# Weight sums used from the tiles they are made in, their raw words loaded on another queue, and their decoding dealt over all bursts

## The chip, the cores and the metric

The kernel runs on one core of a Trainium2 chip. The metric is the device time of the execution in microseconds (us). The engines are named as in the profile: PE (TensorE, with PEld for its weight loads), DVE (VectorE), ACT (ScalarE), POOL (GpSimd) and SP (SyncE, which here only issues DMAs). Each takes its instructions in the order of the program. PE's granted clock has two levels, 2.4 GHz (shown as 1.00) and 1.2 GHz (0.50).

## The reference

```python
# 8 batches, 12 heads, 448 tokens, head size 64
scores = q @ k.T / sqrt(64) - log(448)
attn = sigmoid(scores) @ v              # (8, 12, 448, 64)
x = attn as (3584 tokens, 768)
a = x @ w1;  b = x @ w2                 # each (768, 1024)
h = (a * b) @ w3                        # (1024, 1024)
out = h @ w_out                         # (1024, 768)
```

q, k and v are float32. The four weights come as 64-bit floating point numbers, which the kernel reads as pairs of 32-bit words and turns into float32 itself.

## The kernel before, in words

**Attention** is worked through in 84 bursts of two items each (the loop over `k` at the end of the first half). An item is a tile of scores (line 173, or the short ones of line 183 for the last 64 keys of two pairs of heads), its sigmoid on ACT (line 163), and one burst later its product with v (lines 196 and 204). Score tiles have two PSUM buffers, so the scores of a burst need the sigmoids of the burst before.

**The bilinear stage**, a and b, is computed for groups of two batches (`up(g)`, four groups). The two batches and the two weights form a 2 x 2 block product, which is done with seven products in place of eight. For each of eight blocks of 128 columns (`fc`) `finish_weights` makes seven weight operands from the float32 blocks `b11`, `b21` (w1) and `b12`, `b22` (w2); I call them sums. Each sum is split into a high and a low part: ACT casts (line 66), DVE subtracts (line 67). A product is 9 matmuls on one sum (line 440): three chunks of the inner dimension times three combinations of high and low. PE's results are added up by DVE (line 419) and ACT (lines 448 and 454), and stored to `g_dram`. A group has 56 products, 504 matmuls.

**Group 0** runs beside bursts 25 to 52: every second burst takes a portion of 36 matmuls, four products. Groups 1 and 2 run in one piece after bursts 58 and 70, group 3 at the end. The remaining weights, w3 and w_out, are decoded in `prepare_rest` beside group 1 and later.

**The weights' way.** `prepare_weights` is a generator: each `next` emits one step. Raw words of one block (768 KB, two tiles in turn) are loaded by SP (line 71). ACT takes the magnitude (line 76), DVE runs six steps (lines 83 to 104) per block of w1 and of w2, and after each step some steps of the block before are popped (`pops`): its sums. So each `fc` has 12 decode steps and 11 more. A step stands for one or two DVE operations, and some have one on ACT. In the last decode step (line 104) the raw tile is read for the last time; the load of the next `fc`'s words into it is issued right behind. The magnitude of these words is taken during the following block.

A sum's parts are written to a `wo` tile (four buffers), POOL stores them to `w_dram` (line 339), and `load_weights` loads them back on SP into a ring of six `w` tiles (line 367), five products ahead of their use. If a sum isn't made by then, `load_weights` runs `next(weights)` until it is.

**The order** of all engines is the order in which the code emits. Before burst 25 one or two weight steps follow each burst, and two bursts before 25 five loads are forced. From burst 25 on steps come only beside products: `beside` takes one unit of `change` (the high and low parts of x) or, if none is left, three or four weight steps.

Of the kernel before, what the change touches and what calls it, by code (L numbers as in the profile page):

```python
# [25 lines left out]
def sigmoid_attention_bilinear_ffn(  # L26
# [39 lines left out]
        hi_engine(out=dst_hi, in_=src)  # L66
        lo_engine.tensor_tensor(out=dst_lo, in0=src, in1=dst_hi, op=ALU.subtract)  # L67

    def load_words(src, pool, bufs=2):
        raw = pool.tile([P, *src.shape[1:-1], 2], U32, name="raw", bufs=bufs)  # L70
        nc.sync.dma_start(out=raw, in_=src)
        return raw

    def magnitude(raw, pool, bufs=2):
# [219 lines left out]

    PRODUCTS = ("A11", "S2", "A12", "S3", "S1", "A22", "S4")

    def prepare_weights():

        def load(fc, i):
            return load_words(words((w1, w2)[i], slice(fc * P, (fc + 1) * P)), p1)  # L300

        extras = iter(())
        raw = [load(0, i) for i in range(2)]
        yield
        nxt = magnitude(raw[0], p1, 3)
        for fc in range(NF):
            fs = []
            for i in range(2):
                f = nxt
                pops = ((2, 2, 2, 1, 1, 0), (1, 0, 1, 0, 1, 0))[i]  # L310
                fs.append(f)
                for step, _ in enumerate(decode(raw[i], f)):
                    if step == 4 and (i, fc) != (1, NF - 1):
                        nxt = magnitude(raw[1 - i], p1, 3)
                    if step == 5 and fc + 1 < NF:
                        raw[i] = load(fc + 1, i)
                    yield
                    for _ in range(pops[step]):
                        if next(extras, None):
                            yield  # L320
            take(extras, 100)
            extras = finish_weights(fc, fs)
        while next(extras, None):
            yield

    def finish_weights(fc, fs):

        b11, b21, b12, b22 = (f[:, h * KH:(h + 1) * KH] for f in fs for h in range(2))

        def subtract(name, in0, in1, out=None):  # L330
            if out is None:
                out = p1.tile([P, KH, P], F32, name=name, bufs=1)
            total(out, in0, in1, ALU.subtract)
            return out

        def divide(k, src):
            wo = p1.tile([P, 2, KH, P], F32R, name="wo", bufs=4)
            split(wo[:, 0], wo[:, 1], src, nc.scalar.copy, nc.vector)
            nc.gpsimd.dma_start(out=w_dram[fc * 7 + k], in_=wo.bitcast(F32))  # L339
            stored.add(fc * 7 + k)  # L340

        divide(0, b11)
        yield 1
        t3 = subtract("t3", b22, b12)
        yield 1
        t1 = subtract("t1", b12, b11, b12)
        yield 1
        divide(2, b21)
        yield 1
        t2 = subtract("t2", b22, t1)  # L350
        yield 1
        n4 = subtract("n4", b21, t2, b21)
        yield 1
        for k, src in ((5, n4), (1, t2), (6, b22), (4, t1), (3, t3)):
            divide(k, src)
            yield 1

    RING = 6
    stored = set()
    ring = {}  # L360

    def load_weights(n):
        if n < NG * NF * 7:
            while n % (NF * 7) not in stored:
                next(weights)
            ring[n] = pm.tile([P, 2, KH, P], F32R, name="w", bufs=RING)
            nc.sync.dma_start(out=ring[n].bitcast(F32), in_=w_dram[n % (NF * 7)])

# [8 lines left out]
    def prepare_rest():  # L377

        raw = {}

        def load(i):
            if i < len(jobs):
                raw[i] = load_words(jobs[i][0], p2[0], 4)

        for i in range(3):
            load(i)
        for _ in range(6):
            yield
        f = magnitude(raw[0], p2[0], 3)
        for i, (_, dst) in enumerate(jobs):  # L390
            load(i + 3)
            for step, _ in enumerate(decode(raw.pop(i), f)):
                if step == 4 and i + 1 < len(jobs):
                    following = magnitude(raw[i + 1], p2[0], 3)
                yield
            nc.gpsimd.dma_start(out=dst, in_=f)
            f = following

    def up(g):

        at = {b: slice(b * S, (b + 1) * S) for b in (2 * g, 2 * g + 1)}
        for fc in range(NF):
# [21 lines left out]

            for k, name in enumerate(PRODUCTS):
                n = (g * NF + fc) * 7 + k
                load_weights(n + RING - 1)
                w = ring.pop(n)
                bank, start, stop = ((0, 1, 0), (1, 1, 0), (0, 0, 1), (1, 0, 1),
                                     (2, 1, 0), (3, 1, 1), (2, 0, 1))[k]  # L430
# [6 lines left out]
                for kc in range(KH):  # L437
                    xh, xl = ops[g][name, kc]
                    for m, (i, x) in enumerate(((0, xh), (0, xl), (1, xh))):
                        nc.tensor.matmul(  # L440
                            a, w[:, i, kc], x, start=bool(start) and kc == 0 and m == 0,
                            stop=bool(stop) and kc == KH - 1 and m == 2, skip_group_check=True,
                        )
                        if (kc, m) != (KH - 1, 2):
                            yield
                if k == 0:
                    p = kept("p")
                    nc.scalar.copy(out=p, in_=a)  # L448
                elif k == 1:
                    u2 = kept("u2")  # L450
                    add(u2, a, p)
                elif k == 2:
                    c11 = kept("c11")
                    nc.scalar.copy(out=c11, in_=a)
                elif k == 3:
                    u3 = kept("u3")
                    add(u3, a, p)
                elif k == 4:
                    c22 = kept("c22")
                    add(c22, a, u3)  # L460
                elif k == 5:
                    add(u3, a, u3)
                    leave(2 * g + 1, u3, c22, u3)
                else:
                    add(u2, a, u2)
                    leave(2 * g, u2, c11, kept("c22"))
# [36 lines left out]

    def beside(g, n):

        if not take(change, 1):
            if g == 0:
                take(weights, 3 + n % 5 % 2)
            else:
                take(rest, 2)  # L510

    qks, splits, vvs = {}, {}, {}
    qks[0] = load_pair(0)
# [45 lines left out]

    for k in range(NBURST + 1):  # L560
        if k == CHANGE:
            take(weights, 10 ** 6)
            phase_1.close()
            p2.append(phase_2.enter_context(tc.tile_pool(name="p2", bufs=2, side="right")))
            rest = prepare_rest()
# [19 lines left out]
        for g, (at, end, stride) in enumerate(spans):  # L585
            if k == at:
                filler = up(g)
            if at <= k < end:
                done = k + 1 - at
                if done % stride == 0:  # L590
                    upto, since = (GROUP * i // (end - at) for i in (done, done - stride))
                    take(filler, upto - since + (10 if k == end - 1 else 0))
                if k == end - 1:
                    change = Units(g + 1)
                break
        else:
            if k < spans[0][0]:
                if k > 2:
                    take(change, 2 if k < 10 else 1)
                    take(weights, 1 if 12 <= k < 23 else 2)  # L600
            else:
                take(change, 3 if k < spans[1][0] else 2)
        if k == spans[0][0] - 2:
            for n in range(RING - 1):
                load_weights(n)
        if k == 1:
            idle_products(6)
    take(filler, 7 * KH * 3 - 9)
# [265 lines left out]
```

## Time and profile before

| | us |
|---|---|
| three runs | 1029.62, 1030.95, 1034.69 (median 1030.95) |
| the profiled execution, its time | 1034.27 |
| its span, first to last instruction | 1032.5 |
| PE busy | 986.9 (96%) |
| DVE busy | 654.1 (63%) |
| ACT busy | 405.5 (39%) |
| POOL busy | 84.6 (8%) |
| mean granted clock | 0.975 |

PE is busy for most of the span, but busy includes the time at the lower clock, in which the same matmuls take twice as long. The idle time of PE and the windows at 0.50 are therefore read together, by stage, and the engines' queues tell what stood ahead of the operation that ended an idle time.

### The profile page before, as it was taken

How to read it: one execution, taken by the hardware profiler on the slowest of the kernel's cores; microseconds unless marked ns; L12 is line 12 of the kernel's file. 1: busy time of each engine (PE TensorE's matmuls, PEld its weight loads, DVE VectorE, ACT ScalarE, POOL GpSimd, SP SyncE). 2: the span in 40 equal slices, each digit the busy share in tenths (PEclk: the TensorE clock that was granted, in tenths of full speed). 3: DMA queues.
4: the chain of work that ended last, by engine and by line, in shares of the span. 5: the costliest groups of instructions: out<-in, count | busy, mean ns of one | idle time of the engine just before them, and what ended most of it. 6: DMA issues, size and time to landing. Idle time of an engine off the chain costs nothing.

```text
span 1032.5 us, 14262 instructions
## 1 busy us (share of the span) xinstructions
PE 986.9 (96%) x5246; PEld 763.1 (74%) x5246; DVE 654.1 (63%) x1051; ACT 405.5 (39%) x591; POOL 84.6 (8%) x156
## 2 busy tenths in 40 slices
PE   9999678988889999999999999999999999999998
PEld 4444455655556589994699964789999999999997
DVE  4786766866532878888788845644445566565563
ACT  6876435543534811118511147211223342323230
POOL 0000111211110001110022100000000000000000
PEclk9999888998889999999999999999999999999999
DMA  7748597997875589995599962598833024343412
GB/s 222 227 130 301 203 340 261 301 311 238 292 263 177 181 272 361 379 377 188 178 354 390 333 209 85 169 320 299 284 130 133 1 99 143 107 144 106 143 37 81
DMA packets 111429, 226.40 MB, mean 219 GB/s; under 512 B 10752, under 2 KB 70144, under 8 KB 111360
## 3 DMA queue, kind: packets, MB, share of 16 engines
q1 hardware_dynamic: 100480, 181.44, 52.6%
q0 software_dynamic: 10880, 44.05, 11.0%
q8 instruction: 42, 0.69, 0.3%
q14 instruction: 27, 0.22, 0.1%
HBM read 170.39 MB, written 55.05 MB: 218 GB/s over the span
## 4 chain that ended last, share of the span: by engine, by line
PE 75%; issue 17%; POOL 3%; DMA 2%; DVE 2%; ACT 1%; SPq 0%; POOLq 0%; ACTq 0%
PE up L440 31%; PE up L839 20%; PE av L196 8%; PE sp L173 7%; PE up L714 6%; POOL w_dram L339 2%; PE sp L183 2%; PE av L204 1%; DMA w<-w_dram 1%; POOL g_dram L423 1%; PE up L488 1%; DMA w_dram<-wo 0%; ACT a L163 0%; DVE A L221 0%; DMA qk<-qT 0%
## 5 line engine op out<-in xcount | busy, mean ns | idle before, releaser
L440 PE MATMUL up<-hS,w 128*128 128x448 f32 x768 | 237.5, 370 | 3.4 <-DVE c L419 2.4
L839 PE MATMUL up<-gh,wo 128*128 128x448 f32 x672 | 192.2, 367 | 0.0
L440 PE MATMUL up<-hA,w 128*128 128x448 f32 x576 | 182.0, 370 | 6.3 <-DVE u L419 5.2
L163 ACT ACTIVATE a<-sp,bias 128x896 f32<-128x896 f32 x168 | 161.4, 1007 | 58.7 <-PE sp L173 55.0
L440 PEld LDWEIGHTS up<-hS,w 128*128 128x128 f32 x768 | 145.2, 189 | 25.1 <-issue 5.4
L440 PE MATMUL up<-lS,w 128*128 128x448 f32 x384 | 141.1, 367 | 0.2 <-DVE lS L67 0.2
L196 PE MATMUL av<-a,vv 128*64 128x448 f32 x576 | 135.4, 586 | 0.0
L839 PEld LDWEIGHTS up<-gh,wo 128*128 128x128 f32 x672 | 126.2, 188 | 11.3
L440 PEld LDWEIGHTS up<-hA,w 128*128 128x128 f32 x576 | 109.2, 190 | 25.1 <-issue 8.0
L839 PE MATMUL up<-gl,wo 128*128 128x448 f32 x336 | 123.2, 367 | 0.0
L440 PE MATMUL up<-lA,w 128*128 128x448 f32 x288 | 105.8, 367 | 0.0
L419 DVE TENSOR_TENSOR u<-up,p 128x448 f32<-128x448 f32 x64 | 39.9, 623 | 91.3 <-PE up L440 91.3
L173 PE MATMUL sp<-high 64*128 64x448 f32 x288 | 64.7, 445 | 26.6 <-ACT a L163 26.6
L173 PEld LDWEIGHTS sp<-high 64*128 64x128 f32 x288 | 28.4, 192 | 82.3 <-ACT a L163 61.3
L196 PEld LDWEIGHTS av<-a,vv 128*64 128x64 f32 x576 | 35.4, 142 | 68.1 <-issue 68.1
L448 ACT COPY p<-up 128x448 f32<-128x448 f32 x32 | 17.1, 534 | 171.4 <-PE up L440 158.8
L440 PEld LDWEIGHTS up<-lS,w 128*128 128x128 f32 x384 | 72.9, 190 | 6.2 <-DVE lS L67 0.5
L839 PEld LDWEIGHTS up<-gl,wo 128*128 128x128 f32 x336 | 63.1, 188 | 5.6
L419 DVE TENSOR_TENSOR u<-up,u 128x448 f32<-128x448 f32 x64 | 39.8, 621 | 40.1 <-PE up L440 39.2
L76 ACT ACTIVATE f<-raw 128x768 f32<-128x768 f32 (+2 forms) x48 | 34.3, 716 | 69.0 <-DMA raw<-w 21.3
L67 DVE TENSOR_TENSOR gl<-gf,gh 128x896 fp32r<-128x896 f32 x40 | 41.9, 1086 | 29.5 <-ACT gh L66 29.5
L67 DVE TENSOR_TENSOR low<-qk,high 128x896 fp32r<-128x896 f32 (+1 forms) x49 | 52.5, 1071 | 11.9 <-ACT high L66 10.9
(83 smaller groups left out, 1313.5 us busy)
## 6 DMA issues: line engine op xcount, KB each, us to landing
w<-w_dram SPq DMA_DIRECT2D x224, 384.0 KB, 5.5
w_dram<-wo POOLq DMA_DIRECT2D x56, 384.0 KB, 5.0
gf<-g_dram SPq DMA_DIRECT2D x16, 896.0 KB, 5.4
raw<-w SPq DMA_DIRECT2D x16, 768.0 KB, 6.1
qk<-qT SPq DMA_DIRECT2D x48, 224.0 KB, 4.8
qk<-kT SPq DMA_DIRECT2D x48, 224.0 KB, 5.2
out<-o_sb SPq DMA_DIRECT2D x48, 224.0 KB, 2.0
vv<-vL SPq DMA_DIRECT2D x24, 384.0 KB, 3.7
```

What stands on the lines that cost most here:

```text
L67: lo_engine.tensor_tensor(out=dst_lo, in0=src, in1=dst_hi, op=ALU.subtract)
L76: nc.scalar.activation(f, raw[..., 1].bitcast(F32), AF.Abs, scale=HW_SCALE)
L163: nc.scalar.activation(dst, src, AF.Sigmoid, bias=bias[:n], scale=scale)
L173: nc.tensor.matmul(sp[:, j], k[rows, 1, at:at + P], q[rows, 0], start=m == 0, stop=m == 2)
L183: nc.tensor.matmul(sp[HEADS[u], j], qk[rows, 1, FULL:], qk[rows, 0], start=True, stop=True)
L196: nc.tensor.matmul(acc[cols, :S], vv[:, c, at:at + D], a[:, j], start=u == 0 and c == 0, stop=u == 1 and c == NC - 2,)
L339: nc.gpsimd.dma_start(out=w_dram[fc * 7 + k], in_=wo.bitcast(F32))
L419: nc.vector.tensor_tensor(out=out, in0=a, in1=b, op=ALU.add)
L440: nc.tensor.matmul(a, w[:, i, kc], x, start=bool(start) and kc == 0 and m == 0, stop=bool(stop) and kc == KH - 1 and m == 2, skip_group_ch ...
L448: nc.scalar.copy(out=p, in_=a)
L714: nc.tensor.matmul(acc, a[:, jc], w[:, jc, ms], start=(jc == 0 and m == 0), stop=(jc == NF - 1 and m == 2),)
L839: nc.tensor.matmul(acc, w[:, fc, ms], g[:, fc], start=start and fc == 0 and m == 0, stop=fc == NH - 1 and m == 2, skip_group_check=True,)
```

## The change

Three things change, and they hang together.

- Group 0 takes each sum from the tile in which it is made. There are ten such tiles in one rotation: the six `w` tiles and the four `wo` tiles (`SLOTS`). A sum is emitted only when the product that used its tile ten sums ago has been emitted (`made`, `used`); otherwise the step yields and does nothing. Sums are still stored to `w_dram`, and groups 1 to 3 load them as before. The first five loads of group 1 are issued at the end of burst 52.
- The raw words of w1 and w2 are loaded from POOL's queue. Those of w3 and w_out stay on SP.
- The steps are dealt differently: two after each burst up to 12, one up to 24, then three in each of the bursts 25 to 52, and two beside each product, in addition to a unit of `change`. Among the last five sums those of `t3` and `b22` trade places.

```diff
-    def load_words(src, pool, bufs=2):
+    def load_words(src, pool, queue, bufs=2):
         raw = pool.tile([P, *src.shape[1:-1], 2], U32, name="raw", bufs=bufs)
-        nc.sync.dma_start(out=raw, in_=src)
+        queue.dma_start(out=raw, in_=src)
...
+    POPS = ((2, 2, 2, 1, 1, 1), (1, 0, 1, 0, 0, 0))
...
-            return load_words(words((w1, w2)[i], slice(fc * P, (fc + 1) * P)), p1)
+            return load_words(words((w1, w2)[i], slice(fc * P, (fc + 1) * P)), p1, nc.gpsimd)
...
-                pops = ((2, 2, 2, 1, 1, 0), (1, 0, 1, 0, 1, 0))[i]
+                pops = POPS[i] if fc else (0,) * 6
...
         def divide(k, src):
-            wo = p1.tile([P, 2, KH, P], F32R, name="wo", bufs=4)
-            split(wo[:, 0], wo[:, 1], src, nc.scalar.copy, nc.vector)
-            nc.gpsimd.dma_start(out=w_dram[fc * 7 + k], in_=wo.bitcast(F32))
-            stored.add(fc * 7 + k)
+            m = len(made)
+            while m >= SLOTS and made[m - SLOTS] not in used:
+                yield False
+            n = fc * 7 + k
+            if m % SLOTS < RING:
+                w = pm.tile([P, 2, KH, P], F32R, name="w", bufs=RING)
+            else:
+                w = p1.tile([P, 2, KH, P], F32R, name="wo", bufs=SLOTS - RING)
+            split(w[:, 0], w[:, 1], src, nc.scalar.copy, nc.vector)
+            nc.gpsimd.dma_start(out=w_dram[n], in_=w.bitcast(F32))
+            ring[n] = w
+            made.append(n)
+            yield True
...
-        for k, src in ((5, n4), (1, t2), (6, b22), (4, t1), (3, t3)):
-            divide(k, src)
-            yield 1
+        for k, src in ((5, n4), (1, t2), (3, t3), (4, t1), (6, b22)):
+            yield from divide(k, src)
...
-            while n % (NF * 7) not in stored:
-                next(weights)
...
-                load_weights(n + RING - 1)
+                if g == 0:
+                    while n not in ring:
+                        next(weights)
+                else:
+                    load_weights(n + RING - 1)
...
+                used.add(n)
...
-        if not take(change, 1):
-            if g == 0:
-                take(weights, 3 + n % 5 % 2)
-            else:
-                take(rest, 2)
+        if g == 0:
+            take(change, 1)
+            take(weights, 2)
+        elif not take(change, 1):
+            take(rest, 2)
...
+                if g == 0:
+                    take(weights, 3)
...
+                    if g == 0:
+                        take(weights, 10 ** 6)
+                        for n in range(RING - 1):
+                            load_weights(NF * 7 + n)
...
-                    take(weights, 1 if 12 <= k < 23 else 2)
+                    take(weights, 2 if k < 13 else 1)
...
-        if k == spans[0][0] - 2:
-            for n in range(RING - 1):
-                load_weights(n)
```

Where the instructions stand shows best at three places. In these rows a name is the tile written and, behind the arrow, the tiles read; L is the line, and x2 means two such rows in a stretch.

The first place is ACT beside the third portion, between one pair of sigmoids (`a`) and the next, before:

```order
L163 ACTIVATE a<-sp,bias 128x896 x2
L284 COPY A_1394<-av 128x448
L66 CAST wo<-f 128x384
L76 ACTIVATE f<-raw 128x768
L66 CAST wo<-t_1330 128x384
L454 COPY c_1433<-up 128x448
L66 CAST wo<-f 128x384 x2
L76 ACTIVATE f<-raw 128x768
L66 CAST wo<-t_1307 128x384
L163 ACTIVATE a<-sp,bias 128x896 x2
```

and now, beside the third portion and the burst behind it:

```order
L284 COPY A_1356<-av 128x448
L66 CAST w<-f 128x384
L469 COPY c_1388<-up 128x448
L66 CAST wo<-f 128x384
L76 ACTIVATE f<-raw 128x768
L66 CAST wo<-t_1390 128x384
L163 ACTIVATE a<-sp,bias 128x896 x2
L66 CAST wo<-t_1358 128x384
L66 CAST high<-qk 128x896
L163 ACTIVATE a<-sp,bias 128x896 x2
```

Two magnitudes and five casts stood between two pairs of sigmoids; now there are one magnitude and three casts, and one cast has moved between the next two pairs.

The second place is SP's queue about burst 23 to 26, before (`raw` are the words of w1 and w2, `w` the sums from DRAM, `qk`, `vv` and `vs` attention's inputs):

```order
L367 DMA w<-w_dram 128x768 x5
L71 DMA raw<-w 128x6x256
L139 DMA vv<-vL 128x3x256
L145 DMA vs<-vL 64x128 x2
L367 DMA w<-w_dram 128x768 x4
L131 DMA qk<-qT 128x448
L131 DMA qk<-kT 128x448
L131 DMA qk<-qT 128x448
L131 DMA qk<-kT 128x448
L367 DMA w<-w_dram 128x768
```

and now, at the same place:

```order
L139 DMA vv<-vL 128x3x256
L145 DMA vs<-vL 64x128 x2
L131 DMA qk<-qT 128x448
L131 DMA qk<-kT 128x448
L131 DMA qk<-qT 128x448
L131 DMA qk<-kT 128x448
```

The sums' loads and the raw words are gone from it; attention's inputs stay in their order.

The third place is the start of POOL's queue, before:

```order
L864 MEMSET const-uint8-127 128x1
L870 UNCONDITIONAL_BRANCH
L339 DMA w_dram<-wo 128x768 x14
L423 DMA g_dram<-u_1160 128x448
L339 DMA w_dram<-wo 128x768
```

and now:

```order
L881 MEMSET const-uint8-127 128x1
L887 UNCONDITIONAL_BRANCH
L71 DMA raw<-w 128x6x256 x4
L352 DMA w_dram<-w 128x768 x4
L71 DMA raw<-w 128x6x256
L352 DMA w_dram<-w 128x768 x2
L352 DMA w_dram<-wo 128x768
```

Four raw loads now come first, and the two first of them wait for nothing; on SP they stood behind the first two pairs of `qk` and the first `vv`.

## Rows read from the trace of the kernel before

**Rows 1.** Stages: stretch, length, busy time by engine (instructions), granted clock, DMA share, GB/s

```profile
97.50:357.10 259.60, 227.18 (x1205) 145.47 (x1203) 160.46 (x264) 126.16 (x187) 36.12 (x65) 0.91 0.75 258
357.10:464.50 107.40, 104.93 (x508) 95.45 (x504) 84.56 (x164) 20.79 (x38) 16.05 (x30) 0.98 0.95 340
316.41:330.22 13.81, 13.81 (x82) 9.69 (x80) 2.96 (x4) 6.15 (x8) 0.54 (x1) 1.00 0.70 228
330.22:357.10 26.88, 26.88 (x171) 15.06 (x169) 20.66 (x35) 18.04 (x28) 1.09 (x2) 1.00 0.52 163
```

**Rows 2.** PE in order of time: start, length, operation [idle before, ended by]

```profile
89.19 0.48 PE L173 MATMUL sp<-high 64*128 64x448 f32 x2 [2.10 <-ACT a L163]
...
128.99 0.74 PE L440 MATMUL up<-hA,w 128*128 128x448 f32 x1 [5.24 <-DVE u L419]
...
155.84 0.74 PE L173 MATMUL sp<-high 64*128 64x448 f32 x2 [6.14 <-ACT a L163]
...
242.75 0.74 PE L173 MATMUL sp<-high 64*128 64x448 f32 x2 [4.31 <-ACT a L163]
...
296.45 0.74 PE L173 MATMUL sp<-high 64*128 64x448 f32 x2 [3.64 <-ACT a L163]
```

**Rows 3.** Windows of the lower clock up to 303 us, columns as Rows 1

```profile
90.95:94.37 3.42, 3.42 (x14) 1.01 (x16) 2.54 (x4) 3.42 (x5) 0.00 (x0) 0.50 0.54 166
...
128.50:131.92 3.42, 2.93 (x8) 2.63 (x9) 3.39 (x6) 0.13 (x1) 1.21 (x3) 0.50 0.48 183
152.39:159.23 6.84, 3.39 (x16) 2.18 (x18) 2.52 (x3) 5.57 (x7) 0.54 (x1) 0.50 0.75 258
...
241.14:247.97 6.83, 5.22 (x20) 2.60 (x20) 2.28 (x3) 5.53 (x8) 0.55 (x1) 0.50 0.98 387
...
295.75:302.59 6.84, 6.14 (x25) 2.65 (x26) 1.02 (x2) 4.09 (x5) 0.43 (x1) 0.50 0.66 261
sum 47.87, PE 40.53 PEld 18.42 DVE 21.14 ACT 30.58 POOL 3.27; mean PE 4.50 PEld 2.05 DVE 2.35 ACT 3.40 POOL 0.36
```

**Rows 4.** ACT's waits from 97.5 to 357.1 us: total, times, longest

```profile
ACT f L76 <- DMA raw<-w: 21.3, 3, 8.3
ACT f L76 <- DVE wo L67: 12.1, 8, 3.4
ACT wo L66 <- DVE f L221: 11.7, 4, 4.3
ACT wo L66 <- DMA w_dram<-wo: 7.2, 3, 3.5
```

**Rows 5.** ACT in order of time, one wait on raw words

```profile
153.59 0.89 ACT L76 ACTIVATE f<-raw 128x768 f32<-128x768 f32 x1 [8.31 <-DMA raw<-w]
```

**Rows 6.** DMAs: raw words in the stage; stores by line (size, median to landing)

```profile
DMA to landing us min/median/max: 4.7/6.1/8.0
...
w_dram<-wo POOLq DMA_DIRECT2D x56, 384.0 KB, 5.0
```

**Rows 7.** The start: DVE and SP in order of time, and stretches as Rows 1

```profile
9.21 0.63 DVE L66 CAST high<-qk 128x896 fp32r<-128x896 f32 x1 [3.66 <-DMA qk<-kT]
...
4.46 1.02 SPq L71 DMA_DIRECT2D raw<-w  x2
...
5.00:6.00 1.00, 1.00 (x7) 0.78 (x8) 0.55 (x1) 0.00 (x0) 0.00 (x0) 1.00 1.03 339
8.00:9.00 1.00, 0.97 (x8) 0.19 (x4) 0.00 (x0) 0.94 (x2) 0.00 (x0) 1.00 0.95 276
```

**Rows 8.** POOL and DVE in order of time, about 145 to 147 us

```profile
145.02 0.54 POOL L339 DMA_DIRECT2D w_dram<-wo  x1 [1.43 <-DVE wo L67]
146.83 0.72 POOL L339 DMA_DIRECT2D w_dram<-wo  x1 [1.27 <-DVE wo L67]
...
146.88 0.55 DVE L89 TENSOR_SCALAR f<-f 128x768 f32<-128x768 f32 x1
```

**Rows 9.** DVE by line in the stage: busy, mean ns, idle before

```profile
L93 DVE SCALAR_TENSOR_TENSOR f<-f,raw 128x768 uint32<-128x768 uint32 x12 | 11.4, 954 | 0.2
```

More of the change, by code (lines that the diff above doesn't have):

```diff
@@ L318, in prepare_weights, with one @@
                     for _ in range(pops[step]):
-                        if next(extras, None):
-                            yield
-            take(extras, 100)
+                        yield from one(extras)
             extras = finish_weights(fc, fs)
-        while next(extras, None):
+        for _ in range(sum(sum(pops) for pops in POPS)):
+            yield from one(extras)
+    def one(extras):
+        while not next(extras):
             yield
+        yield
     def finish_weights(fc, fs):
@@ L336, in divide @@
         def divide(k, src):
-            wo = p1.tile([P, 2, KH, P], F32R, name="wo", bufs=4)
-            split(wo[:, 0], wo[:, 1], src, nc.scalar.copy, nc.vector)
-            nc.gpsimd.dma_start(out=w_dram[fc * 7 + k], in_=wo.bitcast(F32))
-            stored.add(fc * 7 + k)
-        divide(0, b11)
-        yield 1
+            m = len(made)
[11 more added lines that the diff above has]
+            yield True
+        yield from divide(0, b11)
         t3 = subtract("t3", b22, b12)
-        yield 1
+        yield True
         t1 = subtract("t1", b12, b11, b12)
-        yield 1
-        divide(2, b21)
-        yield 1
+        yield True
+        yield from divide(2, b21)
         t2 = subtract("t2", b22, t1)
-        yield 1
+        yield True
         n4 = subtract("n4", b21, t2, b21)
-        yield 1
-        for k, src in ((5, n4), (1, t2), (6, b22), (4, t1), (3, t3)):
-            divide(k, src)
-            yield 1
-    RING = 6
-    stored = set()
+        yield True
+        for k, src in ((5, n4), (1, t2), (3, t3), (4, t1), (6, b22)):
+            yield from divide(k, src)
+    RING, SLOTS = 6, 10
+    made, used = [], set()
     ring = {}
@@ L382, in load @@
             if i < len(jobs):
-                raw[i] = load_words(jobs[i][0], p2[0], 4)
+                raw[i] = load_words(jobs[i][0], p2[0], nc.sync, 4)
         for i in range(3):
@@ L561, in sigmoid_attention_bilinear_ffn @@
         if k == CHANGE:
-            take(weights, 10 ** 6)
             phase_1.close()
```

## The prediction, made before the changed kernel was run

> **What bounds the kernel now.** I read the time by stage first [rows 1]. TensorE (PE) is what the end hangs on, so a change can only give back PE's idle time and the time it runs at the lower of its two clock levels. Nearly all of that lies in one stage: 97.5 to 357.1 us, where group 0's matmuls (line 440) are dealt between the attention bursts. PE is idle there for 259.60 - 227.18 = 32.4 us and the mean granted clock is 0.91. In the stage behind it PE waits 107.40 - 104.93 = 2.5 us, although VectorE (DVE) is busy 84.56/107.40 = 79% of it. So DVE's load alone does not stop PE; in the stage in question it is 62%.
>
> The idle time is eleven gaps between 85 and 303 us, ten of them inside the stage; [rows 2] has those that get a term of their own. Behind most gaps the clock then stands at 0.50 for 3.4 or 6.8 us [rows 3]: nine such windows up to 303 us hold 40.53 us of PE work, which at the full level would take half, so they cost 20.3 us, 1.7 of it before the stage. The stage loses 32.4 + 18.6 = 51.0 us. A cross-check: without them it would take 208.6 us. The stage has 14 portions of 36 matmuls, one every second burst; the last two pieces of [rows 1] are free of gaps, from the thirteenth portion to the last one (13.81 us) and from there to the end (26.88 us), and 13 x 13.81 + 26.88 = 206.4.
>
> Who keeps PE waiting? All ten gaps end with a sigmoid (line 163) or with a DVE operation, both in queues that hold weight work too. So I went to ScalarE (ACT) [rows 4]: 21.3 us for raw words of w1 and w2, 23.8 us for DVE's part of the sums, 7.2 us for the store that still reads one of the four buffers. I sort PE's losses by that:
> - raw words late: gaps 5.24, 6.14, 4.31 (ACT's three waits on raw words stand just before them; [rows 5] is the one before 6.14), 15.7 us, and half the busy time in the windows behind them (2.93, 3.39, 5.22), 5.8 us: **21.5 us**.
> - store buffer: gap 3.64 and half of 6.14: **6.7 us**.
> - the rest of the stage, 51.0 - 21.5 - 6.7 = **22.8 us**: ACT and DVE waiting for each other after a clump of weight steps.
> - the gap at 89 us, ahead of the stage, where the first five weight loads force their sums out in one clump: 2.10 + 3.42/2 = **3.8 us**.
>
> **The change part by part.** Raw words. A raw tile is free when the last decode step (line 104) of its chunk is done, and its new words are wanted at the next magnitude (line 76) on that tile. I counted the PE work that the code's order puts between the two (9 matmuls are 1.9 us, a burst 3.2 us). Before, three to four weight steps go into each product and none into bursts, so for four of the eleven loads that fall into the stage only 0 to 3.7 us lie between; a load takes 6.1 us in the median [rows 6], and three of the four are the three waits above. After, the same count gives 8.2 us at the least and 10.6 in the median, because steps come two to a product and three to each burst, and GpSimd's (POOL's) queue holds only stores that wait for DVE, which has passed them by then. What POOL needs to issue such a load isn't in the trace: its stores with one row per partition take 0.54 us [rows 8], a raw load has six. Bounds: 0.54, and 6 x 0.54 = 3.3 us. Landing is then 6.1 to 9.0 us. I take 7, nearest to the store's 5.0 us [rows 6]; even at 9.0 only the loads with 8.2 and twice 8.7 us are late, by under 1 us, which sigmoids have as slack (ACT's wait of 8.31 us cost PE 6.14). So 21.5 us go.
>
> Sums straight from their tiles. 56 loads of 384 KB leave SP; every tile is finished at least 11 us of PE work before its first matmul by the same count, so PE gets no new wait here. The cast into a tile now waits until PE has read that tile ten sums ago. That is enforced in the code order, and ACT, behind PE's sigmoids anyway, finds it done, except inside a portion, where it has time. Ten buffers in place of four: the stores that hold them were issued long before, and the 6.7 us go. Group 1 is loaded from DRAM as before; its first five loads now come at the end of the portion of burst 52, some 19 us ahead of their use: nothing.
>
> Dealing. A portion of 36 matmuls (7.5 us) had about 14 weight steps beside it and now has 8, with 6 in the two bursts. At 0.55 to 0.95 us of DVE work a step [rows 8, 9], with line 419's sums, the code's order put 9 to 14 us of DVE work beside 7.5 us of PE in the dense portions, and now puts 5 to 9. What is then left over at a portion's end falls, by the same count, from 4 to 10 us to 1.5 to 4. It doesn't vanish, so I leave a third of the 22.8 us in place: 15.2 us go; between 8 and 22.8 is possible. The forced clump at 89 us is gone: 3.8 us.
>
> Start. This is what the change costs. The first two raw loads stood on SP behind both pairs of q and k and the first v; now POOL issues them at once. DVE's cast of the second pair starts the moment its k lands, at 9.21 us [rows 7], and PE's short scores wait for the same landing. The DMA engines are full then (shares 1.03 and 0.95). Two loads of 768 KB at 339 GB/s are 4.6 us. If all of that goes ahead, the landing slips by 4.6 us; if POOL's are served last, by 0. I take 3.7: they queue beside each other from the first microsecond, and a part of the raw words still lands after. From there to 97.5 us PE has one gap only, the one counted above, so nothing takes the slip back. A pause this long brings the lower level: the nearest rows, 2.10 and 3.64 us of idle time, go with windows that cost 3.42/2 = 1.7 and 6.14/2 = 3.1 us; I take 2.4. Together **6.1 us lost**, 0 to 8.
>
> The Trainium skill weighs on this at one place: DMA: Bandwidth & Descriptors, section SWDGE vs HWDGE vs iDMA (Issuing engines are not separate DMA queues), says that DMAs from all issuing engines run on the same 16 engines and interleave. By that the slip at the start is there and the sum stays 993; were it otherwise, it would be 987. The trace fits it (the shares of 1.03 and 0.95), but no row has both queues loading in that stretch.
>
> A second rule speaks against the change. A store took 0.72 us in place of 0.54, and beside it ran a DVE operation with one source tile [rows 8]; a raw load with six rows might so lose 6 x 0.18 = 1.1 us, which is inside the bounds above. The Trainium skill, SBUF — State Buffer, section Summary: rules for kernel authors, says that descriptor generation on GpSimd starves while DVE runs in its faster modes, and to issue from another queue. The 0.18 us agrees in kind; by that rule at full weight the slower rival below would hold.
>
> Sum: 21.5 + 6.7 + 15.2 + 3.8 - 6.1 = 41.1 us. The profiled execution took 1034.27 us (span 1032.5), so 993.2; it lies 3.3 us above the median of 1030.95, so I say **990 us** for the median.
>
> **The rivals.**
> - Half of it stays. ACT and DVE still wait for each other at each portion's end, as they did in gaps where no DMA was late, and some raw words come late because the stage is now denser. Raw 13, store 6.7, rest 6, clump 3.8, start 8: 21.5 us gained, 1009. For it: DVE's load rises to 160/213 = 75%. Against: 79% in the stage behind it, with one gap.
> - All of it comes and the start is free: 51.0 + 3.8 = 54.8, 976. For it: PE has filler matmuls at the start. Against: full DMA engines.
> - Slower: POOL's raw loads are the new wait. With landing at 14.5 us all eleven miss their lead by 3.6 us on average, each costing about 2 us of idle time and 2.4 of clock: 48 us, as much as is won. It decides from there on; at 16 us of landing it gives 1047. Against: POOL's stores land in 5.0 us, SP's raw loads in 8.0 at the worst [rows 6].
> - The change does not do what it says: the waits named on ACT were followers, and PE is held by the sigmoid's own turn. Then the gaps stay and only the start is paid, 1030 to 1036. Against: the last two portions before 357 us, which have no weight work beside them, run without a gap.
>
> **How the numbers follow.** Forecast 0.60 (982 to 1002), half 0.18, all and more 0.09, slower by POOL 0.06, no effect 0.07, split between the last two classes. A measurement of this kernel tells about 0.5%, 5 us, from no change. Faster 0.86, same 0.06, slower 0.08. For 8 in 10 the range takes in the lower bound of the start and of the rest at the fast end (978), and half at the slow end: 978 to 1010.
>
> **What would show it.** Right: PE's idle time from the first portion on falls from 32 us to under 8, the clock there is 0.97 or more, no wait of ACT on raw words over 2 us, the landing of the second k near 13 us, one early window at 0.50. Wrong: ACT waits on raw words again (POOL's issue rows over 3 us, landing over 10), casts that wait for PE, or gaps of 2 to 3 us behind every portion.

## The result, and the profile after

The changed kernel takes 989.33 us (median of four runs, 988.64 to 989.85), the kernel before 1032.12 beside it (1029.62 to 1034.69): ratio 0.9585, 95% interval 0.9558 to 0.9612. The forecast was 990 in 978 to 1010. The profiled execution took 988.85 us, its span is 987.1, against 1034.27 and 1032.5: 45.4 us less.

The two stages of [rows 1], from just before the first matmul of group 0 (97.55 us before, 96.99 now) to the start of group 1, and group 1 (columns as there):

```profile
96.95:313.15 216.20, 211.17 (x1205) 139.68 (x1203) 162.06 (x266) 125.46 (x188) 44.60 (x76) 0.99 0.65 217
313.15:418.35 105.20, 102.80 (x508) 94.57 (x504) 84.63 (x164) 20.78 (x38) 16.29 (x30) 1.00 0.96 348
```

The first stage is 259.60 - 216.20 = 43.4 us shorter. PE is idle there for 5.0 us where it was 32.4, and the clock is 0.99 where it was 0.91; the DMA share fell from 0.75 to 0.65 although the stage is shorter. Group 1 is 2.2 us shorter.

PE in order of time, all pauses of over 1 us behind the first matmul (before: [rows 2]):

```profile
11.16 0.97 PE L183 MATMUL sp<-qk 64*64 64x448 f32 x4 [1.94 <-DMA qk<-kT]
...
118.06 0.62 PE L454 MATMUL up<-hS,wo 128*128 128x448 f32 x1 [2.39 <-DVE c L429]
...
204.82 0.47 PE L454 MATMUL up<-hA,wo 128*128 128x448 f32 x1 [1.07 <-ACT p L463]
...
220.28 0.47 PE L454 MATMUL up<-hS,w 128*128 128x448 f32 x1 [1.12 <-DVE c L429]
...
326.96 0.47 PE L454 MATMUL up<-hS,w 128*128 128x448 f32 x1 [2.40 <-DVE c L429]
```

One more, of 1.27 us, waits for a sum from DRAM in group 3. In place of the nine windows at 0.50 up to 303 us [rows 3] there are two:

```profile
12.41:15.82 3.41, 3.41 (x10) 1.26 (x7) 2.09 (x3) 0.77 (x1) 0.00 (x0) 0.50 0.90 314
118.22:121.64 3.42, 3.42 (x10) 3.05 (x11) 2.08 (x4) 0.00 (x0) 0.77 (x2) 0.50 0.40 161
```

The pause at 11 us and the window behind it are new, and are what the change costs at the start. POOL and DVE there, in order of time (before: [rows 7]):

```profile
1.29 0.98 POOL L71 DMA_DIRECT2D raw<-w  x1 [0.85 <-POOLq L881]
9.60 0.85 POOL L71 DMA_DIRECT2D raw<-w  x1 [7.33 <-DMA raw<-w]
...
11.12 0.63 DVE L66 CAST high<-qk 128x896 fp32r<-128x896 f32 x1 [5.64 <-DMA qk<-kT]
```

The second k lands 1.9 us later than before. The second row was in nobody's forecast: nothing in the program makes POOL's second raw load wait, yet it is issued 7.33 us late, 0.3 us after the first has landed (9.29). ACT's waits in the stage (before: [rows 4]) show raw words still late, though half as long:

```profile
ACT f L76 <- DMA raw<-w: 10.3, 4, 4.3
ACT wo L66 <- DVE f L221: 6.0, 3, 3.5
ACT f L76 <- DVE w L67: 4.4, 5, 1.7
```

So two things were to be settled: which of the three parts brings the gain, and what POOL's queue does.

### The profile page after: what moved, and what is told of

The parts are those of the page before. It is cut to its first block, busy times and chain, and to the rows that moved or that the text cites. A ratio compares the mean times of both kernels' runs of the same rounds, so it can differ in the third digit from the quotient of the medians.

```text
span 987.1 us, 14120 instructions
## 1 busy us (share of the span) xinstructions
PE 968.4 (98%) x5246; PEld 757.0 (77%) x5246; DVE 656.1 (66%) x1051; ACT 403.8 (41%) x591; POOL 98.3 (10%) x172
## 4 chain that ended last, share of the span: by engine, by line
PE 84%; issue 5%; DMA 4%; DVE 4%; POOL 1%; ACT 1%; SPq 1%; POOLq 0%; DVEq 0%; ACTq 0%
PE up L454 33%; PE up L856 21%; PE av L196 10%; PE sp L173 9%; PE up L731 7%; DMA w<-w_dram 3%; PE sp L183 2%; PE av L204 2%; POOL w_dram L352 1%; DMA qk<-kT 1%; DMA raw<-w 1%; DVE u L429 0%; DVE A L221 0%; DVE lS L67 0%; ACT a L163 0%
## 5 line engine op out<-in xcount | busy, mean ns | idle before, releaser
L454 PE MATMUL up<-hS,w 128*128 128x448 f32 x702 | 215.9, 368 | 4.8 <-DVE c L429 3.5
L163 ACT ACTIVATE a<-sp,bias 128x896 f32<-128x896 f32 x168 | 160.6, 1006 | 54.3 <-PE sp L173 48.1
L454 PE MATMUL up<-hA,w 128*128 128x448 f32 x522 | 163.5, 367 | 1.4 <-DMA w<-w_dram 1.4
L454 PEld LDWEIGHTS up<-hS,w 128*128 128x128 f32 x702 | 132.0, 188 | 22.2 <-DVE c L429 4.5
L454 PE MATMUL up<-lS,w 128*128 128x448 f32 x351 | 128.5, 366 | 0.2 <-DVE lS L67 0.2
L196 PE MATMUL av<-a,vv 128*64 128x448 f32 x576 | 128.0, 559 | 0.0
L454 PEld LDWEIGHTS up<-hA,w 128*128 128x128 f32 x522 | 98.1, 188 | 14.2 <-issue 3.5
L454 PE MATMUL up<-lA,w 128*128 128x448 f32 x261 | 95.4, 366 | 0.0
L454 PEld LDWEIGHTS up<-lS,w 128*128 128x128 f32 x351 | 66.0, 188 | 5.5 <-DVE lS L67 0.5
L173 PE MATMUL sp<-high 64*128 64x448 f32 x288 | 62.0, 427 | 0.9 <-ACT a L163 0.9
L66 ACT CAST gh<-gf 128x896 fp32r<-128x896 f32 x40 | 35.8, 943 | 60.2 <-PE up L856 50.0
```

What stands on the lines that cost most here:

```text
L163: nc.scalar.activation(dst, src, AF.Sigmoid, bias=bias[:n], scale=scale)
L173: nc.tensor.matmul(sp[:, j], k[rows, 1, at:at + P], q[rows, 0], start=m == 0, stop=m == 2)
L196: nc.tensor.matmul(acc[cols, :S], vv[:, c, at:at + D], a[:, j], start=u == 0 and c == 0, stop=u == 1 and c == NC - 2,)
L454: nc.tensor.matmul(a, w[:, i, kc], x, start=bool(start) and kc == 0 and m == 0, stop=bool(stop) and kc == KH - 1 and m == 2, skip_group_ch ...
```

## The experiments

Ratios are to the kernel before on the same chip, whose median was 1028.9 to 1034.3 us from one set of runs to the next; 0.001 is 1 us.

### Which part does what

The change has three parts, and each was run without the others, or the others without it.

| dealing | tiles | POOL's queue | run | median, us | ratio and 95% interval |
|---|---|---|---|---|---|
| new | yes | yes | the changed kernel | 989.33 | 0.9585 (0.9558 to 0.9612) |
| new | yes | no | e1_raw_sp | 984.55 | 0.9562 (0.9525 to 0.9600) |
| new | yes | no | e12_raw_sp_again | 984.81 | 0.9527 (0.9496 to 0.9557) |
| new | no | no | e4_new_deal | 1002.64 | 0.9739 (0.9684 to 0.9794) |
| old | yes | no | e6_tiles_only | 1015.58 | 0.9836 (0.9792 to 0.9880) |
| old | yes | yes | e3_old_deal | 1016.66 | 0.9876 (0.9837 to 0.9914) |
| old | no | yes | e5_pool_only | 1046.92 | 1.0142 (1.0099 to 1.0186) |

**e1_raw_sp**, POOL's part undone:

```diff
-            return load_words(words(...), p1, nc.gpsimd)
+            return load_words(words(...), p1, nc.sync)
```

> The changed kernel (989.3 us) with the raw words of w1 and w2 issued by SP again; sums from their tiles and the new dealing stay. Theory A, POOL's queue only costs: the second k lands at about 9.1 us again in place of 11.03, the pause of 1.94 us and the window at 0.50 behind it go (3.5 us), and the later raw loads are issued within 1 us of the end of line 104, where POOL issued three of them 3.9 to 7.0 us behind it, so ACT's 10.3 us of waiting for raw words fall under 3 and the pause of 1.07 us at 205 us goes: 989.3 - 3.5 - 1.1 = 984.7 us (984 to 986.5). Theory B, another queue was needed: a raw load that waits for DVE at the head of SP's queue holds attention's q, k and v behind it, PE waits for them, and the time is 990 us or more.

Measured 984.55 us. Theory A holds: the pause ahead of the short scores is 0.40 us, no window follows it, and ACT's waits for raw words are a single one of 2.5 us. One and the same load shows the two queues. First the changed kernel, DVE's last read of a raw tile (line 104) and POOL around the load into it; then the kernel with raw words on SP:

```profile
199.54 0.96 DVE L104 TENSOR_TENSOR f<-f,raw 128x768 f32<-128x768 f32 x1
...
201.70 0.54 POOL L433 DMA_DIRECT2D g_dram<-c  x1
202.23 0.54 POOL L352 DMA_DIRECT2D w_dram<-w  x1
207.48 0.84 POOL L71 DMA_DIRECT2D raw<-w  x1 [4.71 <-DVE wo L67]
```

```profile
194.48 0.96 DVE L104 TENSOR_TENSOR f<-f,raw 128x768 f32<-128x768 f32 x1
...
195.46 0.37 SPq L71 DMA_DIRECT2D raw<-w  x1
```

SP issues it 0.03 us after line 104 ends, POOL 6.98 us after. The releaser that the last POOL row names can't be it: by the program the load waits for line 104 alone.

**e4_new_deal**, the kernel before with the dealing of the change and nothing else:

```diff
-        if not take(change, 1):
-            if g == 0:
-                take(weights, 3 + n % 5 % 2)
-            else:
-                take(rest, 2)
+        if g == 0:
+            take(change, 1)
+            take(weights, 2)
+        elif not take(change, 1):
+            take(rest, 2)
...
+                if g == 0:
+                    take(weights, 3)
...
-                    take(weights, 1 if 12 <= k < 23 else 2)
+                    take(weights, 2 if k < 13 else 1)
```

> The kernel before with the new dealing alone: two steps after each burst up to 12, one up to 24, three in each of the bursts 25 to 52, two beside each product besides a unit of change. Raw words stay on SP, and group 0 loads its sums from DRAM five products ahead. Theory A, the dealing carries it: raw loads have 5.6 us of PE work or more between issue and use, so 21.5 us and 15.2 us go, the store buffers' 6.7 us and the forced clump's 3.8 us stay: about 995 us (992 to 1005). Theory B, the way through DRAM is what holds ACT and DVE (sums forced five products ahead, four buffers held by stores): 1012 us or more.

Measured 1002.64 us: in theory A's range, at its slow end. A's reason does not hold: it had the raw words' waits gone, and ACT still waits 18.0 us for them, in five waits:

```profile
ACT f L76 <- DMA raw<-w: 18.0, 5, 5.6
```

They cost PE less than the three before: it is idle for 12.7 us of group 0's stage in all, where it was 32.4.

**e6_tiles_only** and **e3_old_deal**: the edit of e4_new_deal taken back in the changed kernel, with the raw words on SP and on POOL.

> The changed kernel with the dealing of before: no steps in bursts 25 to 52, three or four beside a product only where no unit of change is left, one or two after the early bursts. Sums from their tiles and POOL's raw loads stay. Theory A, the dealing carries the raw words' 21.5 us and the 15.2 us of clumps: four raw loads have 3.7 to 5.6 us of PE work between issue and use, ACT waits for raw words over 15 us in all, and the time is 1010 to 1028 us. Theory B, the tiles and POOL's queue carry the gain: 1000 us or less.

> The old dealing and SP's raw loads, but group 0 takes its sums from the ten tiles: of the three parts of the change only that one. If the parts add up, it takes what is left of the whole: raw words on SP with both others gain 44.4 us, the dealing alone 26.3, so 18.1 are left: 1011 us (1006 to 1014). It is 5.8 us less than with POOL's queue beside it (1016.7): 4.0 at the start and the rest from raw words that come sooner. If the old dealing leaves the tiles nothing to give (the waits of ACT only change their name), 1022 us or more.

1016.66 and 1015.58 us. The first is inside theory A's range, but not by A's reason: A had ACT wait over 15 us for raw words, and it waits 8.8 us. The second is above its own range (1006 to 1014). The 5.8 us forecast between the two are 1.1 by the medians and 4 by the ratios, which this many runs do not tell apart. In e6_tiles_only the waits for raw words are down to

```profile
ACT f L76 <- DMA raw<-w: 5.7, 2, 3.7
```

(6.8 with one more, which the view gives to DVE although a load landed right before it ended). With raw words on SP throughout, ACT waits for them 21.3 us before, 18.0 with the dealing alone, about 6 with the tiles alone and 2.5 with both. It is the tiles that take most of these waits away, not the dealing. What PE waits for has changed its name in e6_tiles_only (its whole span):

```profile
PE up L454 <- ACT w L66: 7.6, 4, 2.5
PE sp L173 <- ACT a L163: 6.3, 7, 1.6
PE sp L183 <- ACT a L163: 4.3, 1, 4.3
PE up L454 <- ACT wo L66: 4.3, 1, 4.3
```

11.9 us of it are matmuls that find their sum not yet cast. With the old dealing the sums themselves are late.

**e5_pool_only**, the kernel before with the raw loads on POOL (the edit of e1_raw_sp turned round):

> The kernel before with one edit: the raw words of w1 and w2 issued by POOL. Theory A, POOL's queue is a cost by itself: the start slips as in the changed kernel (3.5 us), and since POOL holds a raw load back until all but one of its earlier stores have landed (in the changed kernel up to 7.0 us behind the end of line 104, against 0.03 us on SP), the four loads with 0 to 3.7 us of lead come later than before: 1029 + 3.5 + 2 to 12 = 1034 to 1045 us. Theory B, a queue apart frees SP and helps: 1025 us or less.

1046.92 us, slower by 1.4%: theory A. The time is 2 us above its range, which started from 1029 us; the kernel before took 1034.3 us beside this run, so the loss is 12.6 us, where A had 5.5 to 15.5. ACT's waits for raw words, 21.3 us before, are 28.3:

```profile
ACT f L76 <- DMA raw<-w: 28.3, 4, 8.8
```

Taken together: the dealing alone gives 2.6%, the tiles alone 1.6%, both 4.4 to 4.7%. Within the intervals the two parts add up. POOL's queue gave nothing anywhere: alone it costs 1.4%, in the whole change 0.2 to 0.6% by the ratios (their intervals overlap; the trace names 3.5 us at the start), and beside the tiles alone the runs show no difference that they could tell.

### Why the dealing alone falls short

Stretch 100 to 240 us (columns as [rows 1]) of three kernels, each fence one: the dealing alone, dealing and tiles (e1_raw_sp), and e13_more_traffic, which follows.

```profile
100.00:240.00 140.00, 129.94 (x707) 85.51 (x706) 113.14 (x186) 77.88 (x117) 25.86 (x47) 0.96 0.95 339
```

```profile
100.00:240.00 140.00, 137.12 (x782) 92.47 (x781) 116.82 (x191) 83.54 (x125) 27.27 (x49) 1.00 0.70 236
```

```profile
100.00:240.00 140.00, 130.07 (x719) 87.04 (x719) 109.83 (x180) 76.11 (x114) 25.51 (x46) 0.96 0.98 324
```

The last two numbers are the DMA share and GB/s. With the dealing alone the 56 loads of sums come in a shorter time, and the DMA engines are busy 0.95 of it; raw words land in 6.6 us in the median against 5.7 with the tiles. To see whether that can be the cause, **e13_more_traffic** puts the same number of bytes back without anybody needing them:

```diff
+    junk = dram.tile([NF * 7, P, DM], U32, name="junk")
...
                 if g == 0:
+                    nc.sync.dma_start(out=junk[n], in_=w1[:P, :DM])
                     while n not in ring:
```

> The changed kernel with raw words on SP (984.8 us), and as many transfers added as the tiles spare: beside each of group 0's 56 products SP issues one copy of 384 KB from an input to a place in DRAM that nobody reads. It waits for nothing and nobody waits for it. It tells why the dealing alone gave 26 us and the tiles 18 more. Theory A, the DMA engines: with the dealing alone they were busy 0.95 of 100 to 240 us (0.70 with the tiles), and the sums' loads there made the raw words land in 6.6 us in place of 5.7; so the share rises to 0.9 or more, ACT waits over 8 us for raw words, and the time is 988 to 1002 us. Theory B, the order is what the tiles mend (sums forced five products ahead, four buffers): the copies are paid by nobody, 983 to 987 us.

995.69 us (ratio 0.9649, 0.9618 to 0.9679): theory A, these bytes cost 11 us. Raw words land in 9.2 us in the median, and one of them makes ACT wait 9.55 us; a copy that frees PE's PSUM buffer is queued behind it, so PE stops for 4.99 us. ACT and PE in order of time:

```profile
176.49 0.89 ACT L77 ACTIVATE f<-raw 128x768 f32<-128x768 f32 x1 [9.55 <-DMA raw<-w]
```

```profile
177.85 0.74 PE L456 MATMUL up<-hA,w 128*128 128x448 f32 x1 [4.99 <-ACT p L465]
```

That does not make 11 of the 18 us between dealing alone and dealing with tiles a matter of bytes. The copies run from DRAM to DRAM and the sums from DRAM to a tile, and raw words land later beside the copies (9.2 us) than in e4_new_deal (6.6). Besides, in e4_new_deal ACT is ready for the raw words sooner. One and the same load, in e4_new_deal and then in e1_raw_sp:

```profile
109.53 0.96 DVE L104 TENSOR_TENSOR f<-f,raw 128x768 f32<-128x768 f32 x1
...
110.96 0.39 SPq L71 DMA_DIRECT2D raw<-w  x1
...
118.60 0.90 ACT L76 ACTIVATE f<-raw 128x768 f32<-128x768 f32 x1 [5.61 <-DMA raw<-w]
```

```profile
108.47 0.95 DVE L104 TENSOR_TENSOR f<-f,raw 128x768 f32<-128x768 f32 x1
...
119.54 0.95 ACT L76 ACTIVATE f<-raw 128x768 f32<-128x768 f32 x1 [0.34 <-DVE w L67]
```

From the end of line 104 the load takes 8.0 us to land in the first and 5.8 in the second, but ACT is ready for it (the operation ahead of it in ACT's queue has ended) 2.5 us behind line 104 in the first and 9.8 in the second. For the five loads that ACT waits for in e4_new_deal it is ready 2.5 to 6.0 us behind line 104; for the same five in e1_raw_sp, 4.1 to 9.8. An estimate from these rows: had they landed as fast as in e1_raw_sp (5.5 to 6.5 us), ACT would still have waited about 9 of the 18.0 us. So the order, theory B's cause, seems to have a part in it too, and how the 18 us divide is not shown. The place in SP's queue is the least of it: line 104 ends at most 1.0 us before these loads are issued. The forced clump at 89 us, which costs 1.67 us of pause in e4_new_deal, and the one store-buffer wait of 4.9 us there are further candidates.

### What POOL waits for

**e2_first_sp**: only the first two loads go back to SP.

```diff
-            return load_words(words(...), p1, nc.gpsimd)
+            return load_words(words(...), p1, nc.gpsimd if fc else nc.sync)
```

> The changed kernel with only the first two raw loads issued by SP, behind the q, k and v that stand ahead of them there; the other fourteen stay on POOL. Theory A, the start's loss is the first two loads ahead of the second k: landing at 9.1 us, no pause there and no early window at 0.50, 989.3 - 3.5 = 985.8 us, with ACT's waits for raw words left as they are (about 10 us). Theory B, the loss at the start has another cause (the sums or the dealing): 989 us, the pause at 11 us stays.

984.18 us (ratio 0.9560, 0.9521 to 0.9599), as much as with all of them on SP: theory A, and 1.6 us more than it said (by the ratios the gain over the changed kernel is 2.6 us, by the medians 5.2). So the start is most of what the changed kernel pays for POOL's queue. POOL still issues some later loads up to 4.7 us late here, but ACT waits 4.2 us for them in all, and PE not at all.

**e7_six_pieces** asks what holds POOL's second load back for 7.33 us:

```diff
-        queue.dma_start(out=raw, in_=src)
+        if queue is nc.gpsimd:
+            for c in range(src.shape[1]):
+                queue.dma_start(out=raw[:, c], in_=src[:, c])
+        else:
+            queue.dma_start(out=raw, in_=src)
```

> The changed kernel with each of POOL's raw loads cut in six, one of 128 rows and 128 KB for each chunk of the inner dimension. It tells what made POOL wait 7.33 us for the first raw load before it issued the second. Theory A, rows in flight: 768 + 128 rows were under way at once, 768 + 256 were not, so at the start seven pieces are issued one behind the other and the eighth or ninth waits for the first to land. Theory B, loads in flight: the third or fourth piece already waits. Theory C, bytes: 768 KB + 384 KB were under way at once, so the ten pieces that make 1.25 MB go out without a wait. The time is not the point: 985 to 995 us by all three.

POOL from the start, in order of time (x7 are seven pieces one behind the other):

```profile
1.27 3.86 POOL L73 DMA_DIRECT2D raw<-w  x7 [0.83 <-POOLq L885]
6.50 0.55 POOL L73 DMA_DIRECT2D raw<-w  x1 [1.36 <-issue]
8.21 1.64 POOL L73 DMA_DIRECT2D raw<-w  x3 [1.18 <-issue]
10.31 0.54 POOL L73 DMA_DIRECT2D raw<-w  x1 [0.46 <-issue]
```

Theory A: seven pieces go, the eighth waits. The first piece lands 4.9 us after its issue, at 6.2, the second at 7.9; the eighth and ninth are issued 0.3 us after each. Seven pieces are 896 rows, eight would be 1024; the raw load of 768 rows goes beside one store of 128 (208.32 in the changed kernel, right behind the load) and not beside two. At 201.70 and 202.23 above two stores stand; the first of them lands 5.4 us after its issue, at 207.1, and the load is issued at 207.48. All of POOL's transfers up to group 1 in the changed kernel fit: by their issues and landings never more than 896 rows are under way, and its late raw loads are issued 0.3 to 0.4 us after a landing. Theory B (loads) and C (bytes: the seven are 0.9 MB, and the changed kernel had 1.15 MB under way) fall. The one execution took 983.66 us, though it has the pause at 11 us too; a single execution does not show that pieces are faster. What the trace shows is that a piece does not have to wait for the room of a whole load, and pieces land in 4.4 us in the median.

### Pauses that are left

**e9_best**, **e10_s4_pool** and **e11_first_light** build on e1_raw_sp. e10_s4_pool:

```diff
-        total(a12, a12, xf.pop((g, "S2", kc)), ALU.subtract)
+        engine = nc.gpsimd if g else nc.vector
+        engine.tensor_tensor(out=a12, in0=a12, in1=xf.pop((g, "S2", kc)), op=ALU.subtract)
...
-        turn = name in (("S1", "S2", "S3", "S4") if g == 0 else ("S2", "S4"))
+        turn = name in (("S1", "S2", "S3", "S4") if g == 0 else ("S2",))
```

e9_best has POOL there in group 0 as well, and beside the first four products `take(weights, 1)` for 2; e11_first_light is e10_s4_pool with that dealing.

> The changed kernel with raw words on SP (984.55 us) and two edits against the two pauses that are left of over 2 us: the three subtractions for operand S4 go from DVE to POOL and, from group 1 on, its high parts from DVE to ACT (at the start of group 1 DVE's queue holds three S4 units of 1.64 us ahead of the addition that PE waits 2.40 us for); and beside the first four products one weight step in place of two (2.44 us pause). Theory A, DVE's queue is what these pauses are: both fall under 1 us and the window at 0.50 at group 1's start goes, 2 to 4.5 us: 980 to 982.5 us. Theory B, the additions then wait for POOL or ACT in DVE's place: 984 us or more.

982.93 us (ratio 0.9525, 0.9489 to 0.9562), in neither theory's range but between them. At group 1's start the pause is gone; in the first portion it grew to 3.50 us, since POOL's subtraction stood behind two stores in its queue, the second of which waited for its sum:

```profile
112.36 0.54 POOL L352 DMA_DIRECT2D w_dram<-w  x1 [1.42 <-DVE w L67]
112.92 1.14 POOL L231 TENSOR_TENSOR A<-A,A 128x448 f32<-128x448 f32 x1
...
114.09 0.39 DVE L66 CAST hS<-A 128x448 fp32r<-128x448 f32 x1 [2.14 <-POOL A L231]
```

> The changed kernel with raw words on SP, and from group 1 on operand S4's three subtractions on POOL and its high parts on ACT. The first portion is as in the changed kernel: the POOL subtraction that stood in front of the addition there (DVE waited 2.14 us for it, and PE 3.50) is gone. Theory A, the pauses are DVE's queue: 2.4 us in the first portion as with raw words on SP alone, none over 1 us at group 1's start and no window at 0.50 there: 4 us less than the same kernel without the edit, measured beside it. Theory B, POOL's subtractions slow DVE beside them (1.57 us for an operation of 0.62) so much that the gain is lost: the same time.

> As the kernel with S4 on POOL from group 1 on, and besides one weight step in place of two beside each of the first four products. Theory A, the weight steps ahead of the addition in DVE's queue are the pause of 2.4 us there: it falls under 1.4 us, and the time is 1 to 3 us less than without this edit. Theory B, DVE waits there for ACT's casts, not for its own queue: the pause stays at 2.4 us, the same time.

> The changed kernel with raw words on SP, unchanged from the first time (984.55 us), so that the two kernels built on it are compared with it on the same chip. 984.5 us; if the chips differ in this as the kernel before did (1028.9 and 1034.3 us), up to 5 us off, and then the two others with it.

e10_s4_pool takes 981.13 us (0.9502, 0.9469 to 0.9535), e11_first_light 982.20 (0.9509, 0.9478 to 0.9539), e12_raw_sp_again 984.81. So the S4 edit gives 3.7 us by the medians of six: theory A, and the pause and the window at group 1's start are gone, though the two kernels' intervals overlap. e10_s4_pool is faster than both kernels of this study (its interval lies below 0.9558). Lighter dealing shortens the first portion's pause from 2.39 to 1.90 us, not under 1.4, and its time is the same within the runs' spread; neither theory is borne out whole.

## Why the prediction was right, and where it was not

**The sum.** Forecast 41.1 us for the profiled execution, measured 45.4.

| term | forecast | measured |
|---|---|---|
| stage of group 0: raw words 21.5, store buffer 6.7, dealing 15.2 | 43.4 | 43.4 |
| clump at 89 us | 3.8 | 4.1 |
| start | -6.1 | -3.5 |
| group 1's start and behind | 0 | 1.4 |

The measured terms are slips, that is, how much earlier or later the same operation comes in the second trace: 3.5 us late when the start is over, 0.6 early at the first matmul of group 0. That the first term meets its forecast to the decimal is luck, as its parts show below. The 1.4 us are luck in part: the pause of 2.40 us at the start of group 1 stands in both, the window at 0.50 behind it only before (2.2 us with what hangs on it), and 0.8 come back behind group 1. A third of the 22.8 us was to stay, 7.6; 5.0 us of idle time and 3.42/2 = 1.7 of clock did, 6.7.

**Raw words: the sizes near, two steps wrong.** The count of leads, "8.2 us at the least", holds for nine of the eleven loads: ACT is ready for them 8.4 us or more behind line 104. For the other two it is ready 4.1 and 6.2 us behind, and the first of these still waits 2.5 us with the load on SP. POOL's issue took 0.83 to 0.98 us (bounds 0.54 and 3.3), landing 6.5 us in the median (7 taken). Wrong was also that "GpSimd's (POOL's) queue holds only stores that wait for DVE, which has passed them by then". POOL waited for landings, with the load up to 7.0 us behind line 104, and "no wait of ACT on raw words over 2 us" did not hold (4.3 and 3.9). It hardly cost PE anything, because it ate slack: one pause of 1.07 us follows such a wait. The slower rival was nearer than its 0.06 says: from the end of line 104 to the landing the worst load took 200.50 to 213.38, 12.9 us (the median of the eleven is 8.3), and the rival decided from 14.5 on all of them.

**Which part gives what: the step that failed.** The raw words' 21.5 and 15.2 us, 36.7, were both put down to the dealing; alone it gave 27 (2.6%). The tiles were given 6.7 and, with the forced loads gone, 3.8; alone they gave 17 (1.6%). The step that failed is the reason given for the raw words' leads, "because steps come two to a product and three to each burst": with just that, ACT still waits 18.0 us for raw words, and with the old dealing and the tiles about 6. The tiles were booked as "56 loads of 384 KB leave SP", for the store buffer and the clump, and not for what else goes with them: the bytes (the DMA engines are 0.95 busy in e4_new_deal, and e13_more_traffic shows that such bytes can cost 11 us) and the sums forced five products ahead. How much each of the two gives stays open. That the two errors cancel in the sum is luck.

**Start: the mechanism right, the size too large.** The slip of the landing was taken as 3.7 us, for two loads; it was 1.9, since POOL had only one under way. Pause 1.94 us and window 3.41/2 = 1.7 make 3.6; the slip behind them is 3.5. The Trainium skill, DMA: Bandwidth & Descriptors, section SWDGE vs HWDGE vs iDMA, says that issuing engines are no queues of their own for the 16 DMA engines; the trace agrees: SP's first vv, issued at 1.65 us, lands 8.0 us later, right behind POOL's load; before it took 4.6.

**The rule against the change.** The Trainium skill, SBUF — State Buffer, section Summary: rules for kernel authors, has GpSimd's descriptor generation starve beside DVE's faster modes. The issue rows, 0.98 us at the longest, do not show that; what holds POOL's late loads back is room for rows (e7_six_pieces). Raw words issued by POOL also land later, in 6.5 us against 5.7 by SP, and no run tells why.

**What would show it.** Idle time under 8 us (5.0), clock 0.97 or more (0.99), one early window at 0.50: as said. The second k at 13 us: it was 11. Two of the signs of being wrong are there as well, at a small size: ACT's 10.3 us for raw words, and two casts that wait for PE, 3.7 and 1.8 us, behind which PE has no pause.

## What to carry to other kernels

When steps are dealt more densely, recompute the DMA share of the shorter stage before any term is booked: a transfer that was hidden in a long stage can cost time in the short one, and a reload of what is still on the chip is the first to drop. A queue is more than its order: ask how much of a load it lets under way at once, and put loads that an engine waits for at the very start behind those it needs first. Run each part of a change alone; here one of three cost time, and the total hid it.

## What the runs showed of the hardware

POOL issued loads and stores only up to 896 rows under way, in the units of this kernel (one row per partition and chunk); SP showed no such limit with the same loads: with raw words on SP two of them, 1536 rows, are under way from 4.9 to 12.2 us. In pieces of 128 rows (e7_six_pieces) the worst load of group 0's stage landed 8.8 us behind line 104, as a whole 12.9.

The same pause of 2.4 us is followed by a window at 0.50 in one execution and not in another of the same program. First portion of raw words on SP, two executions (columns as [rows 1]), pauses of 2.44 and 2.39 us ahead:

```profile
114.71:118.12 3.41, 3.41 (x17) 3.16 (x18) 3.30 (x7) 0.00 (x0) 1.19 (x2) 1.00 0.68 249
```

```profile
116.45:119.87 3.42, 3.42 (x11) 3.04 (x11) 3.13 (x6) 0.00 (x0) 1.74 (x3) 0.50 0.52 194
```

Neither of the two pauses of 2.4 us in e2_first_sp is followed by one. By half its length such a window costs 1.7 us; over the one at the start of the changed kernel the slip grew by 1.6. So a pause of this size is a chance of that, not a certainty.

Beside a subtraction on POOL, DVE's operations took up to two and a half times as long (e9_best, 308 to 313 us; the same operations take 1.09 and 0.62 us elsewhere):

```profile
307.38 4.92 POOL L231 TENSOR_TENSOR A<-A,A 128x448 f32<-128x448 f32 x3 [16.28 <-DVE lA L67]
...
309.24 2.04 DVE L67 TENSOR_TENSOR low<-qk,high 128x896 fp32r<-128x896 f32 x1
311.21 1.58 DVE L221 TENSOR_TENSOR S<-A,A 128x448 f32<-128x448 f32 x1
```

The Trainium skill, SBUF — State Buffer, section Who interferes with whom, says that a DVE instruction with two inputs in SBUF and a GpSimd instruction that reads SBUF shut each other out; these rows agree. PE has no pause there all the same: it was not waiting for DVE.
